# Gated attention and hash-routed experts: V becomes the stationary operand, three pairs of groups are turned through transfers

## The chip, the cores and the metric

The kernel runs on one core of one Trainium2 chip. The metric is the device time of one execution in microseconds. The engines are named as in the profile: PE is the matrix engine (PEld its weight loads), DVE the vector engine, ACT the scalar engine, POOL GpSimd, SP the engine whose queue issues most transfers (DMAs).

## The reference

```
scores = (z @ z.T) / S                      # per batch: S=2496, z has 64 columns; symmetric
attn   = maximum(scores, 0) ** 2
x      = u * (attn @ v)                     # u, v: (8, 2496, 256), float32
expert = token_id * 2654435761 % 8          # token_id & 7
out[token] = maximum(x[token] @ w1[expert], 0) @ w2[expert]    # w1: (8,256,1024), w2: (8,1024,256)
```

There are 8 batches (B) and 19968 tokens in all; everything is float32.

## The kernel before

**Tiles and groups.** A batch's 2496 rows are 19 whole tiles of 128 (P) and one last tile `TM` = 19 of 64 rows (R). Four tiles (G) make a group; there are five groups (NG), the last of three and a half tiles. The attention runs over 40 pairs (b, g) of batch and *query* group, in order; for each, over all 20 *key* tiles t. The second half of the program is the expert network: tokens were scattered into expert order in `x_rows`, and blocks of 512 (and partly filled ones of 128) go through w1 (`ups`, L735) and w2 (`down`, L747).

**Sharing by symmetry.** Because the score matrix is symmetric, `scores(b, g)` (L213) makes only key tiles of the own and later groups (`fresh`). The tile `made[b, g, a]` holds keys of group a in its partitions and queries of group g in its columns; ReLU is L221 (ACT, a few on DVE, L219), the square L235 (ACT). For a later query group, `made[b, a, g]` is turned into `mirror[b, a, g]` by DVE transposes of 32x32 blocks, one instruction for each pair of partition quarters (r, c): 16 instructions of 32 partitions x 512 for one pair of groups (`turns_of`, L249). There are ten such pairs a < g in a batch. Within the own group, part of the upper triangle is turned too (`own_turns`, L265): coarse, in steps of two tiles, for g = 0, 1 and fine, in steps of one tile, for g > 1 (`fine`; `skipped` says what is not computed). In batch 0, groups 0 and 1 compute everything.

**The sums.** `attend` (L338) takes a 128x128 piece of the squared scores as the *stationary* operand (`lhs`) and 256 columns of V as the *moving* one; `acc[i // 2][:, i % 2, :]` collects 128 queries x 256 columns for four query tiles i in two PSUM banks. The last key tile has 64 rows and goes through `attend_last` (L330), two halves of the array at once. The 64 queries of the last tile have a copy of their own, `short`, and sums of their own, `attend_short` (L310). A float32 matmul shows as two PE instructions, so counts of PE rows are twice those of matmuls.

**The order** is written by hand. A group starts with two key tiles (EARLY) for query tiles 0, 1, then for 2, 3; then 14 key tiles for all four; then `attend_last`; then all scores of the next group; then the three last key tiles (LATE) for query tiles 0, 1, whose `gate` (L347) follows, then for 2, 3 and their `gate`. `gate` is a DVE instruction that multiplies PSUM by u and 1/S^2 into `x_sb`. There are two accumulators for all groups, so the next group's first matmuls wait for the gate. After each step, `square(2)` issues two squares, `turn_scores` as many pending transposes as a budget of 1450 or 1600 ns per step allows (own group first, nearest pair next), and `between` one small step of other work: routing (`places`), token placement (`enter`), or the scatter of a finished x tile into `x_rows` (`place_x`, L557, an indirect transfer of POOL). `turn_now` issues at once whatever a matmul is about to need.

**Buffers.** Six mirrors (one used by the routing until the third group), seven `a` tiles (`made`), two of V, two of u; SP's queue loads u for the next group, V of the next batch at g = 0 and z of the next batch at g = 2.

**The change-over.** In the last group, mirrors that are free become weight buffers; block 0's w and x are loaded early, the weights of the first partial block (`load_w(NW, 1)`) before the last `attend_last`. `run` then goes through the blocks: `ups` of block i, with `down` of block i-1 between, and `turn_x` (L635), a DVE transpose of the next block's x, in the second bank of each `ups`.

Of the kernel before, what the change touches and what calls it, by code (L numbers as in the profile page):

```python
# [24 lines left out]
def kernel(  # L25
# [42 lines left out]
    c2 = (1.0 / S) ** 2  # L68
# [13 lines left out]
    xpool = pool("xpool", 3)  # L82

# [3 lines left out]


    slot_dram = nc.dram_tensor("slot_tokens", (P * NS,), I32)


    short = const.tile([P, T, R], F32)
    odd = const.tile([R, D], F32)
# [4 lines left out]
    nc.gpsimd.memset(short[R:P, TM, :], 0.0)  # L98
# [24 lines left out]
    zn, zT, v_sb, u_sb, x_sb, made, mirror, to_square, to_turn, gated = {}, {}, {}, {}, {}, {}, {}, [], [], []  # L123
# [24 lines left out]
    def load_v(b):  # L148
        v_sb[b] = vpool.tile([P, T, D], F32, name="v_sb")
        for g in range(NG):  # L150
            tiles_io(vf, b, group(g), v_sb[b][:, g * G:, :], False, nc.sync, twice=True)
# [21 lines left out]

    def whole(g):

        return range(G if g < NG - 1 else G - 1)
# [5 lines left out]


# [9 lines left out]
    def skipped(b, g, t):  # L193

        if t // G != g or b == 0 and not fine(g):
            return 0
        return (t % G if fine(g) else t % G // 2 * 2) * P

    def fine(g):


        return g > 1
# [3 lines left out]
    def scores(b, g):  # L206

        n = sum(width(t) for t in group(g))
        for k, t in enumerate(fresh(b, g)):
            lo = skipped(b, g, t)  # L210
            h = ds((t % 2 if t % G < 2 else 1 - t % 2) * K, K)
            ps = mm_ps.tile([P, G * P], F32, name="s_ps", tag="mm")
            nc.tensor.matmul(ps[:, lo:n], zT[b][h, ts(t, P)], zT[b][h, ds(g * G * P + lo, n - lo)], start=True, stop=True)  # L213
            if t % G == 0:
                made[b, g, t // G] = apool.tile([P, G, G * P], F32, name="a", tag="a")
                rooms.append((b, g, t // G))
            a = made[b, g, t // G][:, t % G, lo:n]
            if k % 2 if (b, g) == (0, 0) else k % 8 == 7 and g == 0:
                nc.vector.tensor_scalar_max(a, ps[:, lo:n], 0.0)  # L219
            else:  # L220
                nc.scalar.activation(a, ps[:, lo:n], AF.Relu)  # L221
            to_square.append((b, g, t))
            if (b, g, k) == (0, 0, T // 2):
                square(EARLY)

    def square(n):
        for b, g, t in to_square[:n]:
            a = made[b, g, t // G][:, t % G, :]
            m = len(whole(g)) * P
            lo = skipped(b, g, t)  # L230
            pairs = [(a[:, lo:m], a[:, lo:m])] if lo < m else []
            if m < G * P:
                pairs.append((short[0:width(t), t, :], a[0:width(t), ds(m, R)]))
            for o, x in pairs:
                nc.scalar.square(o, x)  # L235
            if t % G == G - 1 and (t // G > g or b or fine(g)):
                turns = turns_of(b, g, t // G) if t // G > g else own_turns(b, g)
                to_turn.extend((n, (b, g, t // G), f) for n, f in turns)

                to_turn.sort(key=lambda e: min(e[1][2] - g, 2 if fine(g) else 1))  # L240
        del to_square[:n]


    def turns_of(b, a, g):

        def turn(r, c, m):
            if (b, a, g) not in mirror:
                mirror[b, a, g] = mirrors.pop(0)
            nc.vector.transpose(  # L249
                mirror[b, a, g][ts(c, Q)].rearrange("p t s q -> p (t s) q")[:, 0:m, ts(r, Q)],  # L250
                made[b, a, g][ts(r, Q)].rearrange("p t (s q) -> p (t s) q", q=P)[:, 0:m, ts(c, Q)])
        for r in range(NQ):
            for c in range(NQ):

                m = (len(group(g)) if r * Q < width(group(g)[-1]) else G - 1) * G
                yield m * Q, lambda r=r, c=c, m=m: turn(r, c, m)

    def own_turns(b, g):
# [7 lines left out]
        for r in range(NQ):  # L266
            for c in range(NQ):
                i, o = ts(r, Q), ts(c, Q)
                if g < NG - 1:
                    yield move(tiles[o, 2:4, 0:2, ts(r, Q)].rearrange("p s i q -> p i s q"), tiles[i, 0:2, 2:4, ts(c, Q)], 4)  # L270
                    if fine(g):
# [4 lines left out]
                if c * Q < R:  # L276

                    yield move(tiles[o, 3, 0:2, ts(r, Q)], short[i, ds(g * G, 2), ts(c, Q)], 2)
                    yield move(tiles[ds(R + c * Q, Q), 3, 2, ts(r, Q)], short[i, g * G + 2, ts(c, Q)], 1)
# [3 lines left out]
    def turn_scores(steps):  # L283
# [3 lines left out]
        turned += steps * (1600 if i >= SORT else 1450)  # L287
        while to_turn and turned > 0:
            n, _, f = to_turn.pop(0)
            f()  # L290
            turned -= n + 170
        turned = min(turned, 0)

    def turn_now(key):
        for e in [e for e in to_turn if e[1] == key]:
            to_turn.remove(e)
            e[2]()

    def lhs(b, g, t, i):

        if t in fresh(b, g):
            return made[b, g, t // G][:, t % G, ts(i, P)]
        return mirror[b, t // G, g][:, i, t % G, :]

    def attend_short(b):

        ps = mm_ps.tile([P, D], F32, name="q_ps", tag="mm")
        for t in range(T):
            a = short[:, t, :] if t in fresh(b, NG - 1) else lhs(b, NG - 1, t, G - 1)[:, 0:R]
            nc.tensor.matmul(ps[ds(t % 2 * R, R), :], a, v_sb[b][:, t, :],  # L310
                             start=(t < 2), stop=(t >= T - 2), skip_group_check=True)
        return ps

    def gate_short(b, ps):
        nc.scalar.copy(odd[:], ps[R:P, :])
        x = x_sb[b, NG - 1] = xpool.tile([P, G, D], F32, name="x_sb")
        nc.vector.tensor_add(odd[:], odd[:], ps[0:R, :])
        nc.vector.scalar_tensor_tensor(out=x[0:R, G - 1, :], in0=odd[:], scalar=c2, in1=u_sb[b, NG - 1][0:R, G - 1, :],
                                       op0=OP.mult, op1=OP.mult)
        gated.append((b * T + TM, x[0:R, G - 1, :]))  # L320

    def attend_last(b, g, acc):

        turn_now((b, TM // G, g))
        for i in (0, 2, 1, 3):
            if i in whole(g):
                h = ds(i // 2 * R, R)
                nc.tensor.matmul(acc[i // 2][:, i % 2, :], lhs(b, g, TM, i)[h], v_sb[b][h, TM, :],  # L330
                                 start=False, stop=False, skip_group_check=True)

    def attend(b, g, k, acc, queries):
        t = summed(b, g)[k]
        turn_now((b, t // G, g))
        for i in queries:
            if i in whole(g):
                nc.tensor.matmul(acc[i // 2][:, i % 2, :], lhs(b, g, t, i), v_sb[b][:, t, :],  # L338
                                 start=(k == 0 and i % 2 == 0), stop=(k == TM - 1), skip_group_check=True)

    def gate(b, g, i, acc):
        if i not in whole(g):
            return
        if (b, g) not in x_sb:
            x_sb[b, g] = xpool.tile([P, G, D], F32, name="x_sb")
        x = x_sb[b, g]
        nc.vector.scalar_tensor_tensor(  # L347
            out=x[:, i, :], in0=acc[i // 2][:, i % 2, :], scalar=c2, in1=u_sb[b, g][:, i, :],
            op0=OP.mult, op1=OP.mult,
        )  # L350
        gated.append((b * T + g * G + i, x[:, i, :]))
# [28 lines left out]
    def places():  # L380

        with tc.tile_pool(name="route", bufs=1) as route:
# [20 lines left out]
            room = sorting[:].rearrange("p t s q -> p (t s q)")  # L403
# [15 lines left out]
            yield  # L419
# [3 lines left out]
            yield  # L423
# [144 lines left out]
    nc.scalar.copy(odd[0:1, 0:1], zero[0:1, 0:1])  # L568
# [4 lines left out]
    load_v(0)  # L573
    load_tokens()
    load_u(0, 0)
# [7 lines left out]
    groups = [(b, g) for b in range(B) for g in range(NG)]  # L583
    place = places()
# [3 lines left out]
    def between():  # L588

        nonlocal i  # L590
        if i < SORT:
# [28 lines left out]
    def load_w(j, k):  # L620
        w1[j] = w_buf[2 * k][:].rearrange("p a b c -> p (a b c)").rearrange("p (h f) -> p h f", h=DP)
        w2[j] = w_buf[2 * k + 1][:].rearrange("p a b c -> p (a b c)").rearrange("p (c d) -> p c d", c=FP)
# [15 lines left out]
    mirrors = [mpool.tile([P, G, G, P], F32, name=f"m_{k}") for k in range(NG * NG // 4)]  # L638
# [3 lines left out]
    for n, (b, g) in enumerate(groups):  # L642
        if n + 1 < len(groups):
            load_u(*groups[n + 1])
        if g == 0 and b + 1 < B:
            load_v(b + 1)
        if g == 2 and b + 1 < B:
# [4 lines left out]
        acc = [acc_ps.tile([P, 2, D], F32, name="acc", tag="acc") for _ in range(2)]  # L652
        for k in range(2):
            for t in range(EARLY):
                attend(b, g, t, acc, [2 * k, 2 * k + 1])
# [3 lines left out]
        for t in range(EARLY, TM - LATE):  # L659
# [17 lines left out]
            attend(b, g, t, acc, range(G))  # L677
# [6 lines left out]
        if g == NG - 1:  # L684
            gate_short(b, attend_short(b))
            if n + 1 == len(groups):
                load_w(NW, 1)
# [12 lines left out]
        for k in range(2):  # L700
            for t in range(TM - LATE, TM):
                attend(b, g, t, acc, [2 * k, 2 * k + 1])
            for q in (2 * k, 2 * k + 1):
                gate(b, g, q, acc)
# [4 lines left out]
    assert not to_turn and next(place, None) is None and i > SORT + 4 * C  # L709
    while gated:  # L710
# [54 lines left out]
    def run(work, first, last, loads, later=None):  # L765

        for i in range(first, last + 1):
# [3 lines left out]
            banks = [*range(BLK // P * 2 if work[i] < NW else 2)] if i < last else []  # L771
            up = ups(work[i]) if i < last else None
            for k in banks:
                next(up)
                if k == 1 and AHEAD <= i + 1 < max(last, loads):
# [15 lines left out]
    NM = len(work) - 3  # L791
    load_x(work[1], 1)
# [45 lines left out]
```

## Time and profile before

| what | value |
|---|---|
| median of 3 runs | 2654.0 us (2653.68 to 2654.44) |
| profiled execution, its own time | 2655.11 us |
| its span, first to last instruction | 2653.2 us |
| PE busy | 2643.0 us, 12054 instructions |
| DVE busy | 1394.5 us, most of it before 1530 us |
| attention ends, expert network begins | about 1533.5 us |

PE's share of busy time does not say how fast it goes: the rows of a matmul overlap[...] (a 256-column row lasts 380 ns, while the next starts after 216 ns). The distance from start to start is read from a merged row of the timeline: its length less one row's, divided by the count less one.

### The profile page before, as it was taken

What the parts mean: (1) busy time and instruction counts of PE and PEld (TensorE: products, weight loads), DVE (VectorE), ACT (ScalarE), POOL (GpSimd) and SP (SyncE); (2) the same over time, 40 slices, a digit from 0 to 9 for tenths busy, and PEclk for the clock granted to TensorE, in tenths of its full rate; (3) what the DMA queues carried; (4) which work ended last, traced back from release to release, by engine and by line L of the source; (5) the groups of instructions that cost most, each with busy time, mean ns of one, the idle gap of its engine ahead of it and who ended that gap; (6) DMA issues with size and microseconds to landing.
All of it is one profiled execution on the core that took longest, in us unless ns stands there. A gap on an engine that the chain in (4) does not pass through costs nothing. (4 is left out here: it accounts for less than half of the span.)

```text
span 2653.2 us, 32524 instructions
## 1 busy us (share of the span) xinstructions
PE 2643.0 (100%) x12054; PEld 2072.2 (78%) x12054; DVE 1394.5 (53%) x2907; ACT 598.1 (23%) x1304; POOL 495.9 (19%) x512
## 2 busy tenths in 40 slices
PE   9999999999999999999999999999999999999999
PEld 7788888888888888888878867777777777777777
DVE  7987888878878877887869811111111111111111
ACT  5115214222233133133142111111111111111111
POOL 1322122212221222222200111111111111111112
PEclk9999999999999999999999999999999999999999
DMA  4212112201220221112101276666666666666662
GB/s 167 63 32 71 39 30 70 51 21 67 51 71 17 51 71 39 37 63 52 33 18 31 63 184 165 162 156 161 154 155 157 155 152 165 164 165 163 166 156 84
DMA packets 288992, 256.74 MB, mean 97 GB/s; under 512 B 179100, under 2 KB 251821, under 8 KB 288832
## 3 DMA queue, kind: packets, MB, share of 16 engines
q1 hardware_dynamic: 268096, 213.55, 32.1%
q0 software_dynamic: 20736, 41.09, 4.6%
q8 instruction: 96, 1.57, 0.3%
q14 instruction: 64, 0.52, 0.1%
HBM read 208.91 MB, written 47.09 MB: 96 GB/s over the span
## 5 line engine op out<-in xcount | busy, mean ns | idle before, releaser
L249 DVE STREAM_TRANSPOSE m<-a 32x512 f32<-32x512 f32 (+1 forms) x1280 | 865.1, 676 | 21.0 <-ACT a L235 0.9
L338 PE MATMUL acc<-v_sb,a 128*128 128x256 f32 x3472 | 764.9, 380 | 0.0
L338 PEld LDWEIGHTS acc<-v_sb,a 128*128 128x128 f32 x3472 | 656.2, 190 | 96.9 <-issue 6.7
L741 DVE TENSOR_SCALAR hT<-h_ps 128x512 f32<-128x512 f32 x161 | 111.4, 692 | 946.2 <-PE h_ps L735 924.1
L735 PE MATMUL h_ps<-v_sb,m 128*128 128x128 f32 (+1 forms) x2080 | 567.7, 431 | 1.5 <-PEq L799 1.5
L747 PE MATMUL o_ps<-m,hT 128*128 128x256 f32 x2576 | 566.3, 379 | 0.0
L747 PEld LDWEIGHTS o_ps<-m,hT 128*128 128x128 f32 x2576 | 486.9, 190 | 77.6 <-issue 14.4
L338 PE MATMUL acc<-v_sb,m 128*128 128x256 f32 x2304 | 504.6, 380 | 2.8 <-DVE x_sb L347 2.8
L735 PEld LDWEIGHTS h_ps<-v_sb,m 128*128 128x128 f32 x2080 | 317.6, 191 | 235.6 <-issue 230.6
L338 PEld LDWEIGHTS acc<-v_sb,m 128*128 128x128 f32 x2304 | 438.7, 190 | 63.6 <-DVE x_sb L347 3.6
L221 ACT ACTIVATE a<-s_ps 128x512 f32<-128x512 f32 (+3 forms) x456 | 205.4, 592 | 851.1 <-PE s_ps L213 851.0
L557 POOL DMA_INDIRECT x_rows<-x_sb,slot_i x160 | 156.2, 976 | 1064.1 <-DVE x_sb L347 886.4
L759 POOL DMA_INDIRECT out_dram<-o_sb,idx x157 | 153.4, 977 | 918.1 <-ACT o_sb L754 910.1
L235 ACT ACTIVATE a<-a 128x512 f32<-128x512 f32 (+3 forms) x472 | 232.8, 651 | 0.0
L265 DVE STREAM_TRANSPOSE a<-a 32x128 f32<-32x128 f32 (+1 forms) x992 | 221.6, 248 | 8.8
L213 PE MATMUL s_ps<-zT 64*128 64x512 f32 (+1 forms) x960 | 195.0, 545 | 0.3 <-ACT zT L171 0.3
L754 ACT COPY o_sb<-o_ps 128x256 f32<-128x256 f32 x161 | 59.9, 372 | 595.4 <-PE o_ps L747 595.4
L739 ACT ACTIVATE hT<-h_ps 128x512 f32<-128x512 f32 x161 | 96.1, 597 | 368.8 <-PE h_ps L735 362.0
L213 PEld LDWEIGHTS s_ps<-zT 64*128 64x128 f32 x960 | 120.3, 186 | 71.2 <-issue 41.5
L545 POOL DMA_INDIRECT slot_tokens<-token,addr x160 | 156.1, 976 | 74.8 <-issue 48.5
L347 DVE SCALAR_TENSOR_TENSOR x_sb<-acc,u_sb 128x256 f32<-128x256 f32 x152 | 57.8, 420 | 194.3 <-PE acc L338 194.1
L635 DVE STREAM_TRANSPOSE v_sb<-v_sb 128x1024 f32<-128x1024 f32 (+1 forms) x65 | 53.9, 829 | 3.6 <-DMA v_sb<-x_rows 3.5
(101 smaller groups left out, 293.4 us busy)
## 6 DMA issues: line engine op xcount, KB each, us to landing
m<-in_moe_w_dram SPq DMA_DIRECT2D x260, 256.0 KB
m<-in_moe_w_dram SPq DMA_DIRECT2D x65, 1024.0 KB
v_sb<-in_v_dram SPq DMA_DIRECT2D x32, 512.0 KB
u_sb<-in_u_dram SPq DMA_DIRECT2D x32, 512.0 KB
v_sb<-x_rows SPq DMA_DIRECT2D x128, 128.0 KB
zn<-in_z_dram SPq DMA_DIRECT2D x28, 304.0 KB
v_sb<-x_rows SPq DMA_DIRECT2D x132, 32.0 KB
x_rows<-zero SPq DMA_DIRECT2D x8, 512.0 KB
```

The lines of the kernel that those rows point to most:

```text
L213: nc.tensor.matmul(ps[:, lo:n], zT[b][h, ts(t, P)], zT[b][h, ds(g * G * P + lo, n - lo)], start=True, stop=True)
L221: nc.scalar.activation(a, ps[:, lo:n], AF.Relu)
L235: nc.scalar.square(o, x)
L249: nc.vector.transpose(mirror[b, a, g][ts(c, Q)].rearrange("p t s q -> p (t s) q")[:, 0:m, ts(r, Q)], made[b, a, g][ts(r, Q)].rearrange("p ...
L265: return n * Q, lambda: nc.vector.transpose(out, in_)
L338: nc.tensor.matmul(acc[i // 2][:, i % 2, :], lhs(b, g, t, i), v_sb[b][:, t, :], start=(k == 0 and i % 2 == 0), stop=(k == TM - 1), skip_gr ...
L545: st = nc.gpsimd.indirect_dma_start(out=slot_dram[:, None], out_offset=bass.IndirectOffsetOnAxis(ap=addr[0:n, c:c + 1], axis=0), in_=token ...
L557: st = nc.gpsimd.indirect_dma_start(out=x_dram[:, :], out_offset=bass.IndirectOffsetOnAxis(ap=slot_i[0:width(c % T), c:c + 1], axis=0), in ...
L735: nc.tensor.matmul(ps[:, ts(i, n)], w1[j][:, c, ts(k * m + i, P)], xT[j][:, :, c, :], start=(c == 0), stop=(c == DP - 1))
L741: nc.vector.tensor_scalar_max(o, ps[:], 0.0)
L747: nc.tensor.matmul(ps[:], hT[j][f][:, ts(t, P)], w2[j][:, f, :], start=(f == 0), stop=(f == FP - 1))
L759: st = nc.gpsimd.indirect_dma_start(out=out[:], out_offset=bass.IndirectOffsetOnAxis(ap=rows, axis=0), in_=o, in_offset=None, bounds_check ...
```

## The change

**Sums.** V is now the stationary operand: even columns of V (`h::2` with h = 0) for `acc[0]`, odd ones for `acc[1]`. The squared scores move, 512 queries at once; in the last group 448 queries, as two pieces of 256 and 192. `acc[h]` holds 128 columns of V by up to 512 queries. `short`, `attend_short` and `gate_short` go; the last tile's 64 queries are columns like the others. 1/S moves into the square. `mirror` is laid out by quarters of queries, so that a moving operand is read in runs of 32 elements.

**Gate.** For each half, DVE turns `acc[h]` in blocks of 32x32 into `x_q` (each second element); after the second half four transfers write it to DRAM (`x_way`), four more read it back as rows of x three steps later (`rows_of_x`), POOL multiplies by u (DVE in the very last group), and then x is scattered as before.

**Turning.** Pairs (0,2), (0,4) and (1,3) of each batch are *carried*: for each column quarter c one DVE transpose of 128 partitions x 512 goes into a `stage` tile, where blocks are turned but stand in the wrong partition quarter; three transfers on SP's queue bring them to the right one, and a copy on ACT, issued three steps later, does the fourth. At most one such step goes in every second step of the order.

**Own sharing** is fine for all groups of the batches after the first, and coarse for group 1 of batch 0. **Loads** move: u of a group at its own ninth key step, V of the next batch in five parts, z at g = 3. The budget of `turn_scores` is 1300 or 1450 ns. The routing gets four more empty steps. At the **change-over**, the weights of the first partial block are loaded after all x writes, its `turn_x` follows the last bank of block 0, and all of block 0's `down` come before the partial block's `ups`.

The diff, cut to its core:

```diff
     def skipped(b, g, t):
-        if t // G != g or b == 0 and not fine(g):
+        if t // G != g or (b, g) == (0, 0):
             return 0
-    def fine(g):
-        return g > 1
+    def fine(b, g):
+        return b > 0 or g > 1
...
-            for o, x in pairs:
-                nc.scalar.square(o, x)
+            a = made[b, g, t // G][:, t % G, skipped(b, g, t):queries(g)]
+            nc.scalar.activation(a, a, AF.Square, scale=1.0 / S)
...
+    CARRIED = {(0, 2), (0, 4), (1, 3)}
     def turns_of(b, a, g):
+        x = made[key][:].rearrange("p t (s q) -> p (t s) q", q=P)
         def turn(r, c, m):
+            o = room()[ts(c, Q), r].rearrange("p i s q -> p (i s) q")
+            nc.vector.transpose(o[:, 0:m], x[ts(r, Q), 0:m, ts(c, Q)])
+        def carry(c):
+            m = room()
+            stage = spool.tile([P, G * G * Q], F32, name="stage")
+            nc.vector.transpose(stage[:].rearrange("p (n q) -> p n q", q=Q), x[:, :, ts(c, Q)])
+            for r in range(NQ):
+                o, y = m[ts(c, Q), r].rearrange("p i s q -> p (i s q)"), stage[ts(r, Q)]
+                if r != c:
+                    nc.sync.dma_start(o, y)
+                else:
+                    to_fetch.append((i + 3, key, lambda o=o, y=y: nc.scalar.copy(o, y)))
...
-                    yield move(tiles[o, 3, 0:2, ts(r, Q)], short[i, ds(g * G, 2), ts(c, Q)], 2)
-                    yield move(tiles[ds(R + c * Q, Q), 3, 2, ts(r, Q)], short[i, g * G + 2, ts(c, Q)], 1)
+                    for h in range(2):
+                        yield move(tiles[ds(h * R + c * Q, Q), 3, 0:3, ts(r, Q)], tiles[i, 0:3, 3, ts(c, Q)], 3)
...
     def attend(b, g, k, acc, halves):
         t = summed(b, g)[k]
         turn_now((b, t // G, g))
-                nc.tensor.matmul(acc[i // 2][:, i % 2, :], lhs(b, g, t, i), v_sb[b][:, t, :],
-                                 start=(k == 0 and i % 2 == 0), stop=(k == TM - 1), skip_group_check=True)
+        for h in halves:
+            for cols, a in squares(b, g, t):
+                nc.tensor.matmul(acc[h][:, cols], v_sb[b][:, t, h::2], a,
+                                 start=(k == 0 and cols.start == 0), stop=(k == TM - 1), skip_group_check=True)
...
+    def gate(b, g, h, acc):
+        n = queries(g) // Q
+        if h == 0:
+            x_q[b, g] = qpool.tile([P, G * NQ, D // NQ], F32, name="x_q")
+        x = x_q[b, g]
+        nc.vector.transpose(x[:, 0:n, h::2], acc[h][:, 0:n * Q].rearrange("p (n q) -> p n q", q=Q))
+        if h == 0:
             return
+        for a in range(NQ):
+            queues[a % 2].dma_start(o[:].rearrange("n p d -> p n d")[:, 0:n, ts(a, D // NQ)], x[ts(a, Q), 0:n])
+        def rows_of_x():
+            for r in range(NQ):
+                queues[r % 2].dma_start(xs[ts(r, Q), 0:m], o[c:c + m].rearrange("i p d -> p i d"))
+            for k, t in enumerate(group(g)):
+                (nc.vector if ends else nc.gpsimd).tensor_mul(y, y, u_sb[b, g][0:width(t), k, :])
+                gated.append((b * T + t, y))
+        to_fetch.append((i + 3, None, rows_of_x))
...
-            for q in (2 * k, 2 * k + 1):
-                gate(b, g, q, acc)
+            gate(b, g, k, acc)
...
+            if first < i == AHEAD:
+                while do:
+                    do.pop(0)()
-                if k == 1 and AHEAD <= i + 1 < max(last, loads):
+                if k == (banks[-1] if i < AHEAD else 0 if i == AHEAD else 1) and AHEAD <= i + 1 < max(last, loads):
                     turn_x(work[i + 1], (i + 1) % LOADS)
...
+    load_w(work[1], 1)
     load_x(work[1], 1)
```

## The prediction

> **What bounds the kernel now.** I read the page's engine totals first, then stretches of time, then the timeline of PE for start-to-start distances, then the groups by shape, then the waits.
>
> ```profile
> PE 2643.0 (100%) x12054; PEld 2072.2 (78%) x12054; DVE 1394.5 (53%) x2907; ACT 598.1 (23%) x1304; POOL 495.9 (19%) x512
> 940.00:1130.00 190.00, 190.00 (x924) 158.25 (x923) 152.93 (x334) 54.57 (x122) 43.98 (x47) 1.00 0.18 49
> 599.80 6.42 PE L338 MATMUL acc<-v_sb,a 128*128 128x256 f32 x29
> 1523.94 3.67 PE L310 MATMUL q_ps<-v_sb,m 128*64 128x256 f32 x32
> 1527.45 1.03 PE L310 MATMUL q_ps<-v_sb,short 128*64 128x256 f32 x8
> 1528.41 1.13 PE L330 MATMUL acc<-v_sb,a 64*128 64x256 f32 x6
> 1529.47 4.15 PE L338 MATMUL acc<-v_sb,a 128*128 128x256 f32 x18
> ```
>
> The second line is one batch (190 us; the columns are PE, PEld, DVE, ACT, POOL, then clock, DMA share and GB/s): PE never idles, DVE works 153 us of it, the others little. The third gives the pace: (6.42 - 0.38) / 28 = 0.216 us from start to start for 256 columns, with a weight load of 0.190 us beside each. So PE's stream of columns is the bound of the attention.
>
> ```profile
> L338 PEld LDWEIGHTS acc<-v_sb,a 128*128 128x128 f32 x3472 | 656.2, 190 | 96.9 <-issue 6.7
> L735 PE MATMUL h_ps<-v_sb,m 128*128 128x512 f32 x1024 | 449.6, 592 | 1.5 <-PEq L799 1.5
> 1571.46 14.03 PE L735 MATMUL h_ps<-v_sb,m 128*128 128x512 f32 x56
> 1585.34 13.98 PE L747 MATMUL o_ps<-m,hT 128*128 128x256 f32 x64
> ```
>
> The expert network has the price of the new form: 512 columns. The third line holds 32 rows of 512 columns and 24 of 128; a stretch of the timeline with 512 alone goes 0.429 us from start to start, against 0.216 (the fourth line: (13.98 - 0.38) / 63). Two of 0.2158 are 0.4315, so a wide instruction saves 2.3 ns over two narrow ones, and no more. There too the moving operand is read in runs of 32 elements, so the new layout of the squares should keep that pace.
>
> **The sums of V.** Before: 8 x 19 x 19 matmuls are 5776 PE rows of 0.2158, 1246.2 us; the short sums take 1528.41 - 1523.94 = 4.47 us a batch, 35.8. Together 1282.0. After: 19 key tiles x 2 halves x 2 rows = 76 rows a group; 32 groups at 0.429 are 1043.8, and 8 last groups at 0.216 + 0.162 (256 and 192 columns; 192 x 0.833 ns + 2.4) are 229.9. Together 1273.7: **-8.3 us**. The last key tile of the last group took 1.06 us for three query tiles, one without a partner; 2 x 0.21 + 2 x 0.16 + 0.1 for the turn of the array's tiling is 0.85: **-1.7** in eight batches.
>
> Here a rule promises far more. The Trainium skill, "TensorE: Matmul & The Clock Gate", Part 3 (What overlaps and what doesn't), says that weight loads overlap running matmuls only where the row group differs. All rows here use all 128 rows; by the rule each load would stand alone, and halving 5776 loads, at the page's estimate of 128 / 1.2 = 107 ns, would save an estimated 309 us. The 0.216 us above leaves no room for a load: 256 columns at the 0.833 ns that the steps between shapes give are 0.213. The row decides; I take nothing for it.
>
> **V's stride.** V is loaded with a step of two elements, and no row shows such a weight load. At no cost: 0. At double: two of the 107-112 ns at which 128-column rows with a load each follow each other (L735's narrow form), 0.22 us, hidden under 0.429 and about under 0.216, not under 0.162: 608 x 0.055 = +33 us. The skill's "SBUF - State Buffer", Door 1, has lines of 16 bytes and asks two hits per line; a step of 8 bytes just makes two. I take 0 and keep 33.
>
> **Own sharing.** Fine instead of coarse saves 256 columns in 14 groups; two tiles share the array, so 2 x 256 x 0.833 / 2 = 0.21 us each, and 0.43 in group 1 of batch 0: **-3.4**.
>
> **The stall in batch 0.**
>
> ```profile
> 98.51 0.76 DVE L347 SCALAR_TENSOR_TENSOR x_sb<-acc,u_sb 128x256 f32<-128x256 f32 x2
> 99.32 1.99 PE L338 MATMUL acc<-v_sb,m 128*128 128x256 f32 x8 [0.37 <-DVE x_sb L347]
> 100.75 2.31 DVE L529 TENSOR_REDUCE slot<-zn 128x160 f32<-128x1280 f32 x1
> 103.78 0.48 PE L338 MATMUL acc<-v_sb,m 128*128 128x256 f32 x1 [2.47 <-DVE x_sb L347]
> 104.00:107.40 3.40, 3.40 (x11) 2.74 (x11) 3.25 (x8) 0.00 (x0) 0.00 (x0) 0.62 0.78 192
> ```
>
> DVE comes late to the gate, a routing reduction falls between the two gates, PE idles 2.84 us, and then its granted clock halves for some 3.4 us (0.62 in the last line), 1.7 more. The four empty steps move that reduction from the gate to the next group's second step, and carrying takes some 15 us off DVE before it, net of group 1's own turning: **-4.0** of 4.5.
>
> **DVE, per batch**: three carried pairs cost 4 x 0.70 (zT's 128x512 transpose, 703 ns) instead of 16 x 0.70, or 10.2 where the last group is in it: -24.2. Fine turning adds 2 x 16 x 0.208 = +6.7; the corner of the last group +0.9; gates: 10 x 0.70 for 19 x 0.42 and 0.83, -1.8. So 153 falls to 134.5 of some 188. This gives no time by itself, since PE is the bound; it is the cover for the rest.
>
> **ACT**: 12 copies of 32x512 at 0.58 (zT's copy) are 7 us a batch against one square fewer per tile of the last group: about 60 of 188. They wait for a stage of three steps (about 5 us) before; behind one that waits stand squares and ReLUs, and then PE. **POOL**: 20 multiplications a batch; its 128x1280 row takes 2.9 us, so 256 elements take between 0.58 and 1.0; I take 0.7, 14 us on top of 44. DVE's transposes kept 703 ns under that row, so I charge DVE nothing. **SP**: 36 carrying and 40 x transfers more a batch, at 0.48 us of issue (four x loads in 1.91), 37 us of queue; 7.5 MB on 9.3 MB, 40 GB/s more, where 194 GB/s were seen. u no longer makes SP stand (378 us in its waits) ahead of the carries, but `rows_of_x` waits for writes, 2 to 4 us, 40 times; behind it are carries and V, and their users are most of a group (38 us) away. z comes one group later, still over a group ahead of its use. Cost 0; without that cover a late mirror stops PE by what it is late.
>
> **The gate** now decides more at once. At a steady handover:
>
> ```profile
> 821.47 0.76 DVE L347 SCALAR_TENSOR_TENSOR x_sb<-acc,u_sb 128x256 f32<-128x256 f32 x2 [5.97 <-PE acc L338]
> 824.06 0.76 DVE L347 SCALAR_TENSOR_TENSOR x_sb<-acc,u_sb 128x256 f32<-128x256 f32 x2 [1.10 <-PE acc L338]
> ```
>
> DVE waits for PE, 5.97 and 1.10 us. After: half 0 ends at 0, half 1 at 2.6 us (6 x 0.429), and PE wants bank 0 again at 2.6 and bank 1 at 2.6 + 4 x 0.429 = 4.3. Gate 1 starts at 2.8 and takes 0.7: done at 3.5, 0.8 us to spare. A transpose out of PSUM with a step of two in its output has no row: 0.70 if it is like zT's, 1.4 if doubled. Both fit (0); at over 1.5 PE waits.
>
> **The change-over.**
>
> ```profile
> 1533.46 17.47 PE L735 MATMUL h_ps<-v_sb,m 128*128 128x512 f32 x64
> 1538.07 3.81 SPq L616 DMA_DIRECT2D v_sb<-x_rows  x8
> 1541.32 0.45 DVE L635 STREAM_TRANSPOSE v_sb<-v_sb 128x256 f32<-128x256 f32 x1 [3.53 <-DMA v_sb<-x_rows]
> 1564.58 3.60 PE L735 MATMUL h_ps<-v_sb,m 128*128 128x512 f32 x8
> ```
>
> Now the last x reaches its loads 4.6 us after PE leaves the attention. After: gate 0.9, writes about 3, reads about 3, four multiplications 1.7, four scatters at 1.28 and 1.5 to land: about 14 us. The partial block is wanted at 13.7 + 13.8 = 27.5 us, the second full block's w1 at 31; its load, issued at about 18 behind 2 MB of other weights, lands near 27. Cost 0 with 4 us to spare; if late, up to 10.
>
> **Sum**: -8.3 - 1.7 - 3.4 - 4.0 = -17.4. On the profiled execution's 2655.1 (span 2653.2 and 1.9 around it) that gives 2637.7; it lies 1.1 over the median of the three runs, so against those 2636.6. I say 2637. From no change this kernel's measurement can tell about 0.2%, 5.3 us.
>
> **Rivals.** *PE's stream alone decides* (2637, 2632 to 2645): 0.70. *Gained, but the change-over is late*: the chain of eight transfers takes 8 us more than counted: 2645, 0.08. *The batch 0 stall stays or another comes in its place, and small waits at the forty handovers eat some*: 2650, 0.10. *The handover turns slower than before*: one mechanism, DVE reaches gate 1 late because its turned stage or PSUM transpose is slow; it decides from 0.8 us of lateness, each 0.1 more costs 39 x 0.1 = 3.9 us, and from 0.6 beyond that the sum is over 2659; at 1 us, 2676. For it: one DVE instruction of 512 takes the place of two of 256, behind up to 1.5 us of turns. Against: the 5.97 us of waiting, and 18 us less work a batch. 0.08. *V's strided load costs double*: 2670, 0.04. That the sums do not become wide can't be: each half is one instruction of 512 columns.
>
> Faster: the first two and a little of the third, 0.79; same 0.09; slower 0.12. The range reaches from 2632 (all stalls of batch 0 gone, a little more at each switch) to 2656.
>
> **What would show it.** L338's successor has 128x512 rows at 0.429 from start to start and half as many weight loads, their idle time grown; DVE at about 135 us a batch; a batch about 1.6 us shorter; no PE wait near 100 us, no granted clock under 1 there; gate transposes near 0.70 us with DVE still waiting for PE before them. Wrong: PE rows that wait for DVE at each group, a 192-column pace over 0.17, or PE waiting for w1 about 31 us after the attention.

## The result and the profile after

| | before | after |
|---|---|---|
| median (6 runs each) | 2653.93 us | 2637.49 us |
| profiled execution: its time, its span | 2655.11, 2653.2 us | 2637.55, 2635.8 us |

The ratio is 0.9939 (95% interval 0.9927 to 0.995): 16.4 us less, with times from 2637.22 to 2638.52. The prediction said 2637.

Where the time went is read from the timeline of PE, by the start of the first scores of batches 1 and 7 and of the first row of the expert network:

| stretch | before | after | difference |
|---|---|---|---|
| start to the scores of batch 1 | 201.65 | 194.77 | -6.88 |
| batches 1 to 6, each | 189.62 | 188.08 | -1.54 (-9.21 in all) |
| batch 7 to the expert network | 194.12 | 192.83 | -1.29 |
| expert network | 1119.76 | 1119.77 | 0.0 |

All of it lies in the attention: 1533.46 us became 1516.08, 17.4 us less. The page's first line, one batch from the view of windows (columns as before), and the groups by shape, after:

```profile
PE 2628.7 (100%) x9494; PEld 1628.7 (62%) x9494; DVE 1229.6 (47%) x2775; ACT 649.0 (25%) x1368; POOL 605.3 (23%) x667
940.00:1130.00 190.00, 190.00 (x612) 104.28 (x611) 131.82 (x317) 60.98 (x130) 58.06 (x66) 1.00 0.35 88
L353 PE MATMUL acc<-a,v_sb 128*128 128x512 f32 x1664 | 728.8, 594 | 0.0
L353 PEld LDWEIGHTS acc<-a,v_sb 128*128 128x128 f32 x1856 | 357.5, 196 | 375.5 <-issue 355.3 <-ACT a L235 5.6 <-ACT m L263 4.4
L370 DVE STREAM_TRANSPOSE x_q<-acc 128x512 f32<-128x512 f32 x64 | 45.9, 718 | 273.9 <-PE acc L353 273.8
L257 DVE STREAM_TRANSPOSE stage<-a 128x512 f32<-128x512 f32 x96 | 67.2, 707 | 2.3
L263 ACT COPY m<-stage 32x512 f32<-32x512 f32 x96 | 59.1, 615 | 403.8 <-DVE stage L257 403.6
L389 POOL TENSOR_TENSOR x_sb<-x_sb,u_sb 128x256 f32<-128x256 f32 x149 | 103.4, 721 | 927.2 <-DMA x_sb<-x_way 927.2
```

PE is still at 190 of 190 us in the batch, with 612 rows for 924; weight loads went from 158 to 104 us, while a batch became only 1.54 us shorter. DVE has 132 us for 153, ACT 61 for 55, POOL 58 for 44. Now PE's timeline in a batch, the stretch of batch 0 where PE had stood, and a steady handover (DVE rows first):

```profile
887.11 20.76 PE L353 MATMUL acc<-m,v_sb 128*128 128x512 f32 x48
...
92.85 5.42 PE L353 MATMUL acc<-a,v_sb 128*128 128x512 f32 x12
98.11 6.17 PE L353 MATMUL acc<-m,v_sb 128*128 128x512 f32 x14
...
95.74 0.72 DVE L370 STREAM_TRANSPOSE x_q<-acc 128x512 f32<-128x512 f32 x1 [4.67 <-PE acc L353]
98.31 0.72 DVE L370 STREAM_TRANSPOSE x_q<-acc 128x512 f32<-128x512 f32 x1 [1.86 <-PE acc L353]
102.23 2.33 DVE L569 TENSOR_REDUCE slot<-zn 128x160 f32<-128x1280 f32 x1
...
884.74 0.72 DVE L370 STREAM_TRANSPOSE x_q<-acc 128x512 f32<-128x512 f32 x1 [7.30 <-PE acc L353]
885.50 1.16 DVE L253 STREAM_TRANSPOSE m<-a 32x384 f32<-32x384 f32 x2
887.32 0.72 DVE L370 STREAM_TRANSPOSE x_q<-acc 128x512 f32<-128x512 f32 x1 [0.66 <-PE acc L353]
```

(20.76 - 0.59) / 47 = 0.429 us from start to start, as priced. In batch 0 DVE now waits for PE at both gates (4.67 and 1.86 us) where PE had waited for DVE. At the steady handover DVE waits 7.30 us before gate 0 but only 0.66 before gate 1, with two turns between the gates.

### The profile page after: what moved, and what is told of

Read it like the earlier page. It is cut to its first block, busy times and chain, and to the rows that moved or that the text cites. A ratio compares the mean times of both kernels' runs of the same rounds, so it can differ in the third digit from the quotient of the medians.

```text
span 2635.8 us, 28491 instructions
## 1 busy us (share of the span) xinstructions
PE 2628.7 (100%) x9494; PEld 1628.7 (62%) x9494; DVE 1229.6 (47%) x2775; ACT 649.0 (25%) x1368; POOL 605.3 (23%) x667
## 5 line engine op out<-in xcount | busy, mean ns | idle before, releaser
L353 PE MATMUL acc<-a,v_sb 128*128 128x512 f32 (+2 forms) x1856 | 766.2, 570 | 0.0
L253 DVE STREAM_TRANSPOSE m<-a 32x512 f32<-32x512 f32 (+1 forms) x896 | 604.0, 674 | 20.3 <-ACT a L235 5.1
L353 PEld LDWEIGHTS acc<-a,v_sb 128*128 128x128 f32 x1856 | 357.5, 196 | 375.5 <-issue 355.3
L353 PE MATMUL acc<-m,v_sb 128*128 128x512 f32 (+2 forms) x1792 | 528.5, 455 | 0.0
L353 PEld LDWEIGHTS acc<-m,v_sb 128*128 128x128 f32 x1792 | 335.1, 196 | 192.4 <-issue 180.5
L389 POOL TENSOR_TENSOR x_sb<-x_sb,u_sb 128x256 f32<-128x256 f32 (+1 forms) x156 | 108.1, 721 | 927.2 <-DMA x_sb<-x_way 927.2
L280 DVE STREAM_TRANSPOSE a<-a 32x128 f32<-32x128 f32 (+2 forms) x1360 | 281.4, 239 | 9.9
L235 ACT ACTIVATE a<-a 128x512 f32<-128x512 f32 (+1 forms) x480 | 227.9, 568 | 0.6
L370 DVE STREAM_TRANSPOSE x_q<-acc 128x512 f32<-128x512 f32 (+1 forms) x80 | 56.3, 704 | 295.1 <-PE acc L353 294.7
L219 PEld LDWEIGHTS s_ps<-zT 64*128 64x128 f32 x960 | 112.0, 186 | 91.2 <-issue 61.0
```

The costliest lines, as they stand in the source:

```text
L235: nc.scalar.activation(a, a, AF.Square, scale=1.0 / S)
L253: nc.vector.transpose(o[:, 0:m], x[ts(r, Q), 0:m, ts(c, Q)])
L280: return n * Q, lambda: nc.vector.transpose(out, in_)
L353: nc.tensor.matmul(acc[h][:, cols], v_sb[b][:, t, h::2], a, start=(k == 0 and cols.start == 0), stop=(k == TM - 1), skip_group_check=True)
```

## The experiments

Differences below are between spans of the profiled executions and the 2635.8 us of the changed kernel; each ratio is to the kernel before, timed beside the same runs. That kernel read 2654.18 us beside runs 1 to 4, 2655.83 beside 5 to 8 and 2655.56 beside 9 to 12, for 2653.93 in the result, so a difference of spans under some 2 us says nothing by itself. The first scores alone start at 8.2 to 9.2 us in different runs (8.85 in the changed kernel). Small differences are therefore read from stretches of the trace between two fixed points.

**1. Narrow moves.**

```diff
-        for r in ([slice(0, NQ)] if TM not in group(g) else [slice(0, R // Q), slice(R // Q, NQ)]):
-            m = G if r.start < R // Q else G - 1
+        for r in ([slice(0, NQ // 2), slice(NQ // 2, NQ)] if TM not in group(g) and t != TM
+                  else [slice(0, NQ)] if TM not in group(g) else [slice(0, R // Q), slice(R // Q, NQ)]):
+            m = G if r.start < R // Q or TM not in group(g) else G - 1
```

> The changed kernel, but in the groups of four whole tiles each move of 512 squares is split into two moves of 256, each loading the same piece of V again (2432 PE rows more). Theory (the stream of columns is all that counts, weight loads lie under it): 2.3 ns for each of 2432 pairs, +5.6 us, about 2643; 256-column rows 0.216 us from start to start. Rival (a load on the same rows of the array stands alone): 2432 loads of 107 ns, +260 us.

2643.57 us (ratio 0.996, 0.9946 to 0.9974), span 2641.8: **+6.0**. A batch goes from 188.08 to 188.83, +0.75. From its source view and PE's timeline:

```profile
L353 PEld LDWEIGHTS acc<-a,v_sb x3520: 193/196/197, 18.0 to 1521.8; 128*128 128x128 f32 x196
911.46 7.07 PE L353 MATMUL acc<-a,v_sb 128*128 128x256 f32 x32
```

The narrow rows follow each other at (7.07 - 0.38) / 31 = 0.216 us, and 2432 loads more, each a row of 196 ns, cost 2.5 ns each: they lie wholly under the stream. The rival is out by a factor of forty.

**2. Own sharing as before.**

```diff
-        if t // G != g or (b, g) == (0, 0):
+        if t // G != g or b == 0 and not fine(b, g):
...
-        return b > 0 or g > 1
+        return g > 1
...
-            if t % G == G - 1 and (t // G > g or not ((b, g) == (0, 0))):
+            if t % G == G - 1 and (t // G > g or b or fine(b, g)):
```

> The changed kernel with the own sharing of before (fine only for groups 2 to 4, nothing shared in groups 0 and 1 of batch 0). Theory: 0.21 us in each of 14 groups and 0.43 in one, +3.4 us, about 2641; DVE about 7 us a batch less. Rival (the finer turning was paid for in waits, so that its gain is gone): within 1 us of 2637.5.

2640.72 us (0.995, 0.9937 to 0.9964), span 2638.6: **+2.8**, and DVE has 4.4 us less to do in the same window of a batch (7 expected). In the trace the gain of the finer sharing is there in full: each batch after the first is 0.42 us longer, and in batch 0 the stretch from the scores of group 1 to those of group 2 is 0.43 us longer, 3.4 us in all. The span shows less because the first scores start 0.5 us earlier here (8.33 us).

**3. No carrying**, at the pace of before.

```diff
-    CARRIED = {(0, 2), (0, 4), (1, 3)}
+    CARRIED = set()
...
-        turned += steps * (1450 if i >= SORT else 1300)
+        turned += steps * (1600 if i >= SORT else 1450)
```

> The changed kernel without carried pairs: all ten pairs are turned on DVE in 16 instructions, with the budget of before (1450 and 1600 ns a step). DVE about 155 us of 188 a batch. Theory (PE's stream is the bound, carrying only makes room): batches 1 to 7 unchanged to 0.5 us each; 0 to 5 us lost in batch 0, where DVE is nearly full: 2637 to 2643. Rival (the new gate needs the room): DVE late at gates, 0.5 us at each of 39 handovers, +20 us, 2657.

2716.58 us (1.0238, 1.0225 to 1.0252), span 2711.4: **+75.5**, and both expectations missed. A batch takes 197.74 us. The waits, and PE's timeline at two of them:

```profile
PE acc L362 <- DVE a L280: 29.0, 8, 4.1
PE acc L353 <- DVE m L253: 18.0, 14, 2.0
...
994.31 0.74 PE L362 MATMUL acc<-a,v_sb 64*128 64x192 f32 x3 [3.76 <-DVE a L280]
1097.04 3.54 PE L353 MATMUL acc<-m,v_sb 128*128 128x512 f32 x4 [1.85 <-DVE m L253]
```

PE hardly waits at the gates (1.7 us in all) but for turned scores that are due: once a batch for the last group's own turns (eight waits), and again for a mirror, 1.85 us in group 2 and 0.51 in the last group. After the two longer waits the granted clock falls as well (0.59 from 994.30 to 997.80, 0.54 from 1097.04 to 1100.40), which makes of some 6 us of waits a batch the 9.7 that it is longer. DVE is busy 148 us of 190 here; it is not full, it is late. So the question became whether pace or deadline makes it late, and which part of the change needs the room (runs 9 and 10).

**4. Routing steps at their old places, carrying kept.**

```diff
-            for _ in range(6):
+            for _ in range(2):
                 yield
```

> The changed kernel with the routing steps at their old places (two empty steps for six), so that the 2.31 us reduction falls between the two gates of group 1 of batch 0 again. Theory (the place of the reduction makes the stall): gate 1 late by 1 to 2 us there, PE waits near 95 us, and the clock may halve after it: +1.5 to +4 us. Rival (carrying alone freed DVE): 0.

2637.85 us (0.9938, 0.9924 to 0.9951), span 2636.4: +0.6. The rival holds:

```profile
96.05 0.72 DVE L370 STREAM_TRANSPOSE x_q<-acc 128x512 f32<-128x512 f32 x1 [4.37 <-PE acc L353]
96.69 2.40 DVE L569 TENSOR_REDUCE slot<-zn 128x160 f32<-128x1280 f32 x1
```

The reduction does fall between the two gates, but gate 0 was on time, and PE loses nothing: from the scores of group 2 to those of group 3 of batch 0 it takes 38.39 us (88.56 to 126.95), and 38.40 in the changed kernel. Batch 0 is 0.3 us longer only because the first scores start that much later.

**5. The kernel before with the six empty steps alone** (the same edit in reverse, on the other kernel).

> The kernel before with one part of the change alone: the routing's four more empty steps. Theory: the reduction leaves the gate of group 1 of batch 0; the first wait of 0.37 us, which comes from DVE being behind, stays, the second of 2.47 us and the halved clock go: -3 to -4 us, about 2650. Rival (DVE is simply full in batch 0, the stall moves elsewhere): within 1 us of 2654.

2654.2 us (0.9994, 0.9986 to 1.0003), span 2652.0, 1.3 under that of before; batch 0 gains 0.7. The 3 to 4 us expected did not come, and the rival holds.

```profile
100.06 0.75 DVE L347 SCALAR_TENSOR_TENSOR x_sb<-acc,u_sb 128x256 f32<-128x256 f32 x2
100.86 3.51 PE L338 MATMUL acc<-v_sb,m 128*128 128x256 f32 x8 [2.01 <-DVE x_sb L347]
```

The reduction is gone from there; DVE reaches gate 0 late anyway, without having waited, and PE stands 2.01 us, after which the granted clock falls (0.55 from 100.86 to 104.30). From the scores of group 2 to those of group 3 it takes 42.54 us, for 43.77 before and 38.58 in a steady batch: 4.0 of the 5.2 us lost there are still lost. With run 4: the stall was a full DVE, not one instruction's place.

**6 and 7. The gate's transpose issued two and three times.**

```diff
-        nc.vector.transpose(x[:, 0:n, h::2], acc[h][:, 0:n * Q].rearrange("p (n q) -> p n q", q=Q))
+        for _ in range(2):    # 3 in run 7
+            nc.vector.transpose(x[:, 0:n, h::2], acc[h][:, 0:n * Q].rearrange("p (n q) -> p n q", q=Q))
```

> The changed kernel with each gate's transpose out of PSUM issued twice (1.4 us for 0.7), to measure the room at the handover. The prediction's sum (0.8 us to spare, both ends counted from PE alone): no wait, 0 to +1 us. Rival (the turns that stand between the two gates are pushed back as well, so that gate 1 ends 0.7 + 0.7 us later): late by up to 0.6 us at each of 39 handovers, +5 to +25 us.

> The changed kernel with each gate's transpose issued three times (2.1 us for 0.7). The prediction's sum: late by 0.6 us at each of 39 handovers, +22 us. Rival (turns between the gates are pushed back too): late by 1.4 to 2.1 us, +55 to +80 us.

2655.89 us (1.0, 0.9992 to 1.0009), span 2654.0: **+18.2**; and 2715.66 us (1.0226, 1.0212 to 1.024), span 2713.0: **+77.2**. By 39 handovers, 0.47 and 1.98 us each. The wait of PE in run 7:

```profile
PE acc L353 <- DVE x_q L371: 60.1, 39, 1.9
```

Every handover is hit, and the rival's sizes hold. In run 6 the profile lists only 13 such waits, 5.6 us, because a short wait hides behind the recorded end of the row before; from start to start every handover is late, by 0.2 to 1.1 us. One of them, the handover into the last group:

```profile
930.81 1.47 DVE L371 STREAM_TRANSPOSE x_q<-acc 128x512 f32<-128x512 f32 x2 [5.62 <-issue]
932.31 1.42 DVE L253 STREAM_TRANSPOSE m<-a 32x512 f32<-32x512 f32 x2
933.76 1.47 DVE L371 STREAM_TRANSPOSE x_q<-acc 128x512 f32<-128x512 f32 x2
935.38 0.84 PE L353 MATMUL acc<-m,v_sb 128*128 128x256 f32 x3 [0.51 <-DVE x_q L371]
```

The doubled gate 0 pushes the two turns, these push gate 1 by some 0.4 us (0.1 where the turns between the gates take 1.16 us), gate 1 itself takes 0.7 longer, and PE goes on 0.15 us after its end (from 933.76 + 1.47 = 935.23 to 935.38). In run 7 both gates are 1.4 us longer, and gate 1 pays for both.

**8. The old order at the change-over.**

```diff
-            if first < i == AHEAD:
-                while do:
-                    do.pop(0)()
...
-                if k == (banks[-1] if i < AHEAD else 0 if i == AHEAD else 1) and AHEAD <= i + 1 < max(last, loads):
+                if k == 1 and AHEAD <= i + 1 < max(last, loads):
```

> The changed kernel with the old order after the attention: the partial block's x is turned in the second bank of the first block, and the first block's down sums come between the partial block's ups. The x chain is as long as now (the turn of the partial block's x at 23 us after the attention's end). Theory (DVE in order: the turn stands ahead of the ReLUs of banks 1, 3, 5, 7 and holds them until x has come): PE runs out of its six banks some 10 us after the attention's end and waits until 23, +8 to +13 us. Rival (PSUM and other work hide it): 0 to 2 us.

2650.32 us (0.9982, 0.9974 to 0.9989), span 2646.7: **+10.9**, of which 9.1 in the expert network's stretch; the other 1.8 lie in the attention, which this edit does not touch (see run 12). DVE holds the ReLUs behind the turn of x, as expected:

```profile
1539.28 0.45 DVE L678 STREAM_TRANSPOSE v_sb<-v_sb 128x256 f32<-128x256 f32 x1 [9.56 <-DMA v_sb<-x_rows]
1539.83 5.17 PE L775 MATMUL h_ps<-v_sb,m 128*128 128x128 f32 x32 [8.07 <-DVE v_sb L678]
```

**9 and 10. No carrying, with less to turn or at a faster pace.** Run 9 is run 3 with the edit of run 2; run 10 is run 3 with 1850 and 1700 for 1600 and 1450.

> The changed kernel without carried pairs, with the pace of before (1450 and 1600 ns a step) and the own sharing of before: DVE has about as much to turn as in the kernel before. Theory (without carrying, the finer own sharing is what no longer fits the pace, so that turns are forced late): the waits of batches 1 to 7 go, 188.5 us a batch, and batch 0 keeps its stall of about 5 us: 2641 to 2646. Rival (the new gate and sums need the room that carrying makes): over 2660.

> The changed kernel without carried pairs, own sharing fine, but a faster pace (1700 and 1850 ns a step). Theory (the pace was the limit, DVE has 40 us idle a batch): waits for mirrors and own turns go, 188 to 189 us a batch, about 2640 to 2650. Rival (more turns stand between the two gates, and gate 1 comes late at each handover): +20 to +60 us over 2637.

Run 9: 2648.67 us (0.9976, 0.9964 to 0.9987), span 2643.5, **+7.6**; 188.77 us a batch, against 188.50 in run 2. The waits of the steady batches are gone, and batch 0 has 3.1 us of its stall again (41.45 us from the scores of group 2 to those of group 3). Its median is 3.5 us over its profiled execution (2645.19, the fastest of seven), and that of run 3 is 3.4 over; why stays open. Run 10: 2658.72 us (1.0011, 1.0004 to 1.0018), span 2656.0, **+20.2**: a batch is 189.49 us, so the faster pace does away with most of run 3's lateness, but batch 0 loses 11.5 us, and the waits are in front of gates:

```profile
PE acc L353 <- DVE x_q L370: 11.5, 13, 6.1
104.69 7.80 PE L353 MATMUL acc<-m,v_sb 128*128 128x512 f32 x13 [6.07 <-DVE x_q L370]
```

Of these 11.5 us, 8.2 lie in batch 0, 6.1 of them before one gate; the steady batches have 3.3, all at the handover into the last group. So neither pace that was tried fits the finer sharing without carrying: the slow one misses deadlines, the fast one puts too much ahead of gates. Carrying takes work off that conflict: DVE is busy 132 us in the window for 148 in run 3, where a batch is 9.7 us longer besides.

**11. Fine sharing in batch 0 as well.**

```diff
-        if t // G != g or (b, g) == (0, 0):
+        if t // G != g:
...
-        return b > 0 or g > 1
+        return True
...
-            if t % G == G - 1 and (t // G > g or not ((b, g) == (0, 0))):
+            if t % G == G - 1:
```

> The changed kernel with own sharing fine in groups 0 and 1 of batch 0 as well: 768 columns fewer in the one, 256 in the other. Theory: -0.64 and -0.21, -0.85 us in the attention stretch (below what the times can tell; the stretch is read from the trace). Rival (DVE, which also does half of the first ReLUs, falls behind in the first 60 us): +1 to +3 us.

2650.19 us (0.9981, 0.9974 to 0.9987), span 2648.3: **+12.4**, 11.7 of it in batch 0; the expected gain of 0.85 is drowned, and the rival's 1 to 3 us were far too few. Around the worst place:

```profile
90.07 0.69 DVE L257 STREAM_TRANSPOSE stage<-a 128x512 f32<-128x512 f32 x1
94.61 1.30 DVE L257 STREAM_TRANSPOSE stage<-a 128x512 f32<-128x512 f32 x2
95.35 1.25 ACT L263 COPY m<-stage 32x512 f32<-32x512 f32 x2 [3.93 <-DVE stage L257]
97.28 3.41 PE L219 MATMUL s_ps<-zT 64*128 64x512 f32 x7 [3.91 <-ACT a L227]
```

The own turns go first and displace a carried pair until its `a` tile must be given to the next scores. Then it is forced: stage, transfer and copy stand in a row on the path, ACT's copies hold up the ReLUs behind them, and PE waits 3.91 us.

**12. V in contiguous halves.**

```diff
-                nc.tensor.matmul(acc[h][:, cols], v_sb[b][:, t, h::2], a,
+                nc.tensor.matmul(acc[h][:, cols], v_sb[b][:, t, ts(h, P)], a,
```

(and the same in `attend_last`)

> The changed kernel with V loaded in two contiguous halves of 128 columns instead of every second column; the output's columns come permuted. Theory (a step of two elements costs the weight load a few ns that lie under the stream): loads 190 ns as before instead of 196, start to start unchanged at 429, 216 and 162 ns, span within 0.5 us of 2635.8. Rival (the step holds up the 192-column rows): these fall below 162 ns and the span by over 1 us.

The output's columns come permuted, so this run serves its times alone. One execution, 2638.68 us, span 2637.0, 1.2 over the changed kernel (the expectation allowed 0.5).

```profile
L353 PEld LDWEIGHTS acc<-a,v_sb x1856: 186/190/190, 18.1 to 1516.9; 128*128 128x128 f32 x186
```

The loads take 190 ns for 196, and rows follow each other at 429, 216 and 162 ns in both kernels. The step costs 6 ns of a load that nothing waits for. Nor does the 1.2 us come from the sums: most stretches between two groups' scores are 0.01 to 0.02 us shorter than in the changed kernel, and the excess lies at the ends of some batches, mainly in scores, as in the first line below. Run 8, whose attention is not edited, has it too (second line); in the changed kernel these 40 rows take 8.11 us (third line). What causes it is open.

```profile
1135.77 8.82 PE L219 MATMUL s_ps<-zT 64*128 64x512 f32 x40
383.26 8.85 PE L219 MATMUL s_ps<-zT 64*128 64x512 f32 x40
1135.17 8.11 PE L219 MATMUL s_ps<-zT 64*128 64x512 f32 x40
```

No run beats the changed kernel.

## Why the prediction was right, point by point

- **The sum: right, and in part by luck.** Of the 17.4 us by the trace, the stall of batch 0 is 5.2 (4.0 counted), the sharing 3.4 (3.4), and what remains for the sums 8.8 (10.0). Two errors of 1.2 us cancel.
- **PE's stream is the bound, loads lie under it: shown.** Run 1 puts 0.75 us a batch on the width (0.70 counted). The rule that the prediction quoted, that loads on the same rows stand alone, does not hold here: 0.216 us from start to start is all that 256 columns with a load of 190 to 196 ns take, before and in run 1. Its 309 us were also counted too high: the loads of the sums fell from 5776 to 3648, not to half, which at the same 107 ns is 228 us.
- **The sums, -8.3 and -1.7.** A steady batch gained 1.54, of which 0.42 is the sharing (run 2): 1.12 for the sums, for 1.25 counted. The term that was wrong is the last key tile (-0.21 a batch). PE's timeline of before shows why: the row that I took to be without a partner was followed by a score row that shared the array with it,

```profile
1149.18 0.91 PE L330 MATMUL acc<-v_sb,a 64*128 64x256 f32 x5
1149.72 0.69 PE L213 MATMUL s_ps<-zT 64*128 64x512 f32 x1
1149.93 0.38 PE L330 MATMUL acc<-v_sb,a 64*128 64x256 f32 x1
```

  so there was little to save: from the start of this tile to the first sums behind the scores it is 9.21 us before (1338.80 to 1348.01) and 8.91 after (1134.30 to 1143.21), and 0.21 of that is the sharing, which leaves 0.09. The lone row that I had read was the very last group's, which no scores follow.
- **Own sharing, -3.4: shown** at 3.4 in the stretches of run 2, but not free as the prediction had it. It fits only because carrying makes room: without carrying, at the old pace, it costs 68 us (run 3 against run 9).
- **The stall of batch 0, -4.0.** From the scores of group 2 to those of group 3 it is 43.77 us before (88.90 to 132.67) for 38.58 in a steady batch: 5.2 us for the stall and the slower clock behind it, 4.5 counted. After it is 38.40, as in a steady batch, so all of it went. The size was near; the cause half wrong. The four empty steps, which the prediction named first, are worth nothing there with carrying (run 4) and 1.2 of 5.2 us without the rest of the change (run 5); without carrying, 3.1 us stay (run 9). What counts is how much DVE has to do before that gate.
- **"This gives no time by itself" (carrying): half right.** The prediction did call it the cover for the rest, which it is, but gave that cover no size: it looked at DVE's mean, 153 of 188 us. Deadlines and gates decide: without carrying, the rest of the change is 75 us slower at the old pace and 20 at a faster one. The sum came out because carrying's value is in stalls that never arose.
- **The gate: no wait, as said, but the room was overrated.** The 0.8 us to spare are in the trace of a handover between full groups: gate 1 ends at 887.32 + 0.72 = 888.04, and bank 1 is wanted at 887.11 + 4 x 0.429 = 888.83. The sum left out that PE goes on only 0.15 us after the gate, that the turns between the gates belong to the chain once gate 0 is longer, and that the last group, with its 256 and 192 columns, wants bank 1 after 4 x (0.216 + 0.162) = 1.5 us and not 1.7. So a transpose of 1.4 us, which the prediction had fit with 0.1 to spare, costs 18 us (run 6). The rival that ended slower had its mechanism right and its threshold too high.
- **The change-over: cost about 0, with no room left.** From the timeline after,

```profile
1516.08 13.90 PE L775 MATMUL h_ps<-v_sb,m 128*128 128x512 f32 x32
1521.25 0.78 SPq L385 DMA_DIRECT2D x_sb<-x_way  x2
1530.45 0.93 POOL L597 DMA_INDIRECT x_rows<-x_sb,slot_i  x1 [0.30 <-issue]
1535.65 3.99 SPq L659 DMA_DIRECT2D v_sb<-x_rows  x8
1547.69 3.67 PE L775 MATMUL h_ps<-v_sb,m 128*128 128x512 f32 x8 [0.33 <-DMA m<-in_moe_w_dram]
```

  the loads of x go out 19.6 us after the attention, not 14: the last scatter, issued at 1530.45, let them go 5.2 us later (1.5 counted), with the DMA engines fully busy at first (share 1.10 from 1530.45 to 1533.00). w1 came at 31.6 us for 31 wanted, and PE waited 0.33 us for it. The 4 us to spare did not exist; 27.5 us for the partial block did hold, and only in the new order (run 8).
- **Durations without a row**: gate transpose 718 ns (700 taken, 1400 feared), POOL's product 721 (700), ACT's copy 615 (580), the strided load free (33 us feared).

## What to carry to other kernels

Price a wider instruction by the distance from start to start of a row that already has the width: 2432 more weight loads, of 196 ns each in the profile, cost 2.5 ns each here. A helper engine at 80% of busy time can still set the time, through deadlines and through what stands in its queue ahead of a handover; relief for it is worth nothing until something else takes up the room, and then it carries the whole change. Room at a handover is measured by lengthening the handover itself: one transpose more in each gate cost 0.47 us a handover, two cost 1.98.

## What had not been expected of the hardware

- A weight load with a step of two float32 elements takes 196 ns and a contiguous one 190 (the changed kernel and run 12), at the same distance from start to start.
- After a wait of PE of only about 2 us the granted clock fell for some microseconds: in run 5 the wait of 2.01 us was followed by eight rows at about 0.427 us for 0.216, some 1.7 us more than the wait itself. The waits of 1.85 us in run 3 were followed by it too (0.54 from 1097.04 to 1100.40), while 39 waits of up to 1.94 us in run 7 left the mean clock at 1.000. So the length of the wait alone does not decide; what else does is open.
- A scatter's rows could be read only 5.2 us after its issue with the DMA share at 1.10 and 2 MB of weights issued 5 to 8 us earlier; before, with a share of 0.29, it was 2.4 (1535.63 to 1538.07). In run 8 it was 3.6 (1532.36 to 1535.93) behind the same weights, so the traffic may not be all of it; no run tested it.
